# A gated linear attention and Mamba kernel: all transfers on one queue, issued by runs, and the weight check read again later

## The chip, the cores and the metric

The kernel runs on one core of a Trainium2 chip. The metric is the device time of one execution in microseconds; before the change it is 334.77 us (median of 3 runs, 333.81 to 335.59). The profile is one execution with a span of 334.8 us.

## The reference

```
# attention: batch 4, heads 8, seq 768, head_dim 48
for t in range(S):
    state = alpha[:, :, t, :, None] * state + np.einsum('bhd,bhe->bhde', k[:, :, t], v[:, :, t])
    y[:, :, t] = np.einsum('bhd,bhde->bhe', q[:, :, t], state)
# x: (4, 768, 384), the heads side by side; then the gated state space block
proj = x @ w_in                       # w_in 384 x 1024, float64
val, gate = proj[..., :512], proj[..., 512:]
h = a[0, 0] * h + val[:, t, :]        # one scan over t for each channel, a = exp(A_log)
out = (silu(gate) * h) @ w_out        # w_out 512 x 384, float64
```

Inputs q, k, v and alpha are float32; the two weight matrices come as float64, so each weight has 8 bytes, which the kernel turns into float32 itself with integer operations.

## The kernel before

**Tiles.** The sequence of each batch is cut into NG = 3 groups of 256 steps, so there are N = 12 groups ("turns" n = 0 to 11), three for each of the four batches. Within a group the recurrence is rewritten with running products of alpha: `front(n)` (L308) makes products V and P with scans on the vector engine (DVE; L339, L344), scales q and k by them (L353, L359), multiplies K and Q in blocks (sc, L368), masks (A, L371) and transposes K back (tpk, L142; copied to Kn by the scalar engine, ACT). `back(n)` (L385) makes block states z (L154) from Kn and v, adds them up to S_n (L393, L402), makes y from A and v (L169) and from S_n and Q (L187), copies y to x_sb on ACT (L410, L412), and transposes it (tpx, L196; copied to xT, L197). `ssm(n)` (L107) is the second block: four times the projections pj (L115, the value half and the gate half), the scan hh on DVE (L119), silu sg on ACT (L124), the product f on DVE (L125), and then twice the output product o (L130), copied to o_sb by ACT (L133) and stored.

**How q, k and alpha come in.** They have to lie with channels on partitions. For groups 0 to 3 they come as rows into the tile pads and are transposed by the matrix engine (tp, L326). For groups 4 to 11 they come as a batch (`load_batch`, L234): for each of a, q and k, several transfers copy 32x32 blocks, in memory runs of 32 or 16 numbers (128 or 64 bytes), and DVE transposes each block (`squares`, L329 and L330). Batch 1 is 48 transfers of 512 runs each; batches 2 and 3 are 12 transfers of 3072 runs each. The tiles of two batches share two buffers: batches 1 and 3 use big0, which at the start holds `staging`, the raw weights; batch 2 uses big1, which at the start holds pads.

**The weights.** 12 "units" (8 of w_in, 4 of w_out, 384 KB each) are fetched raw into staging (`fetch_unit`), and `convert_unit` (L270) makes float32 of each on ACT (L276, L277), DVE (L278, L280) and GpSimd (POOL, L282). The conversion holds only for weights in a certain range of size; `check_units(p)` (L284) tests that on ACT, three units at a time in place in staging, by a Square pass (L288) and a Relu pass (L289) with their sums in left_w. `check_products` (L377) tests the products V in the same manner. At the end `any_outside` reduces all of this to a flag; if it is set, a second slower program, `general`, runs. With these inputs it doesn't.

**What sets the order.** The order of each engine's instructions is written by hand: a string of letters for each turn. F steps front(n), A steps front(n+1), B steps back(n), P and H step ssm(n-1) (matmuls, then scan, silu and product), O steps ssm(n-2), which by then has only its two output products left, C checks products, U converts a unit, W checks units, L and M issue transfers:

```
467  early = ["FFFFLUFUFABBABB", "UUFPUUFHPUHFFPUHBBCPHABUAUBL", "FPUFHPUHFFPHBBCAPHBWAWOBWAWOM"]
468  usual = "FLPHPHFFOABBCPHABPHBAOM"
469  ending = ["PHPHOPHPHO", "OO"]
```

Each engine executes its instructions in this order, and each waits for its inputs and for its buffers. Transfers are issued by the sync engine (SP), which does nothing else, or by ACT, in whose stream an issue stands between computations. Before, SP issues pads, weights, the first four v and the batches; ACT issues the store of each o_sb (L134) and v of turns 4 to 11 (`load_last`, L483). `load_later` (L474) issues batches 2 and 3 at L of turns 3 and 5, and `load_last` batch 1 at M of turn 2, the whole batch at once. Pools matter too: the transposes tp, tpk and tpx share two PSUM buffers (ps_tp), pj and o share two (ps_mm), o_sb and xT have two each, v has three.

Of the kernel before, what the change touches and what calls it, by code (L numbers as in the profile page):

```python
# [9 lines left out]
FP32 = mybir.dt.float32  # L10
U8 = mybir.dt.uint8
U32 = mybir.dt.uint32
# [6 lines left out]
def kernel(  # L19
# [24 lines left out]
    nc = tc.nc  # L44
    B, H, S, D = q.shape
    DM = H * D
    DI = moe_A_log.shape[0]
    C = 128
    R = 64
    NR = C // R  # L50
    G = 2
    GC = G * C
    GR = G * NR
    NG = S // GC
    NP = H // 2
    DP = 64
    GP = G * NP
    NK = DM // C
    NI = DI // C
    N = B * NG  # L60
# [12 lines left out]
    w_out = const.tile([C, NI, DM], FP32, name="w_out")  # L73

    left = const.tile([C, N, 2], FP32, name="left")
    WP = 3
    left_w = const.tile([C, 3 * NI // WP, 2], FP32, name="left_w")
    flag = const.tile([1, 1], I32, name="flag")
    bias = const.tile([C, 3], FP32, name="bias")
# [3 lines left out]
    units = []  # L83
# [7 lines left out]
    def load_heads(dst, src, n, queue=nc.sync):  # L91

        b, g = divmod(n, NG)
        for c in range(G):
            rows = ds(g * GC + c * C, C)
            queue.dma_start(out=dst[:, c], in_=src[b, :, rows, :].rearrange("h p d -> p h d"))

    def load_pairs(dst, src, n, queue=nc.sync):

# [7 lines left out]
    def ssm(n, xT, prev_h, pool, ps_mm):  # L107

        b, g = divmod(n, NG)
        f = pool.tile([C, NI, GC], FP32, name="f")  # L110
        for cc in range(NI):
            pj = ps_mm.tile([C, 2, GC], FP32, tag="mm", name="pj")
            for i in range(2):
                for kk in range(NK):
                    nc.tensor.matmul(pj[:, i, :], w_in[:, kk, i, ds(cc * C, C)], xT[:, kk, :],  # L115
                                     start=(kk == 0), stop=(kk == NK - 1))
            yield
            hh = pool.tile([C, GC], FP32, tag=f"h{cc}", name="hh")
            nc.vector.tensor_tensor_scan(  # L119
                out=hh, data0=a_dec[:, cc:cc + 1].to_broadcast([C, GC]), data1=pj[:, 0, :],  # L120
                initial=prev_h[cc][:, GC - 1:GC] if g else 0.0, op0=ALU.mult, op1=ALU.add)
            prev_h[cc] = hh
            sg = pool.tile([C, GC], FP32, name="sg")
            nc.scalar.activation(sg, pj[:, 1, :], AF.Silu)  # L124
            nc.vector.tensor_mul(f[:, cc, :], sg, hh)  # L125
            yield
        for c in range(G):
            o = ps_mm.tile([C, DM], FP32, tag="mm", name="o")
            for cc in range(NI):
                nc.tensor.matmul(o, f[:, cc, ds(c * C, C)], w_out[:, cc, :],  # L130
                                 start=(cc == 0), stop=(cc == NI - 1))
            o_sb = pool.tile([C, DM], FP32, name="o_sb")
            nc.scalar.activation(o_sb, o, AF.Copy)  # L133
            nc.scalar.dma_start(out=out[b, ds(g * GC + c * C, C), :], in_=o_sb)  # L134
            yield

    def keys_back(K, Kn, ps_tp):
# [66 lines left out]
    def ranged(ctx):  # L204
        def pool(name, bufs, **kw):
            return ctx.enter_context(tc.tile_pool(name=name, bufs=bufs, **kw))

        own = pool("own", 1)
        p1 = pool("p1", 1)
        p2 = pool("p2", 2)  # L210
        p3 = pool("p3", 3)
# [18 lines left out]
        W = 32  # L230
        NW = S // W
        batches = {}

        def load_batch(b):  # L234
            t = big.tile([C, 3, NP * NW * W], FP32, tag=f"big{1 - b % 2}", name="batch")
            for m, (name, src) in enumerate((("a", alpha), ("q", q), ("k", k))):
                tv = t[:, m].rearrange("p (x e) -> p x e", e=W)
                batches[b, name] = t[:, m].rearrange("p (j x) -> p j x", j=NP)
                w0 = max(0, BY_VECTOR - NG * b) * GC // W
                for i in range(2):  # L240
                    nc.gpsimd.memset(tv[ds(DP * i + W, W), :, D - W:W], 1.0 if name == "a" else 0.0)  # L241
                for j, nj in [(0, NP)] if w0 == 0 else [(j, 1) for j in range(NP)]:
                    for i in range(2):
                        for half in range(2):
                            ch = min(W, D - W * half)
                            nc.sync.dma_start(  # L246
                                out=tv[ds(DP * i + W * half, W), j * NW + w0:(j + nj) * NW, 0:ch],
                                in_=src[b, ds(NP * i + j, nj), w0 * W:S, ds(W * half, ch)]
                                .rearrange("j (w p) d -> p (j w) d", p=W))

        vs, st, xs = {}, {}, {}

        def load(n, names="aqkv", queue=nc.sync):
            for name in names:
                if name == "v":
                    vs[n] = p3.tile([C, G, H, D], FP32, name="v_sb")
                    load_heads(vs[n], v, n, queue)
                elif n < BY_VECTOR:
                    load_pairs(pads[n % NBUF][name], dict(a=alpha, q=q, k=k)[name], n, queue)

        staging = big.tile([C, len(units), NK * C * 2], U32, tag="big0", name="staging")
# [19 lines left out]
                                           op0=ALU.bitwise_and, op1=ALU.bitwise_or)  # L281
            nc.gpsimd.tensor_add(units[u][0].bitcast(I32), units[u][0].bitcast(I32), lo.bitcast(I32))  # L282

        def check_units(p):  # L284


            h = staging[:, ds(WP * p, WP), :].rearrange("p u (x two) -> p (u x) two", two=2)[:, :, 1].bitcast(FP32)
            nc.scalar.activation(h, h, AF.Square, scale=2.0 ** -16, accum_out=left_w[:, p, 0:1])  # L288
            nc.scalar.activation(h, h, AF.Relu, scale=-2.0 ** 60, bias=bias[:, 0:1], accum_out=left_w[:, p, 1:2])  # L289

# [86 lines left out]
        def check_products(n):  # L377
            V = Vs[n % 2]
            junk = p1.tile([C, NP, GC], U8, name="junk")
            nc.scalar.activation(junk, V[:, :, 0:GC], AF.Relu, scale=-1.0 / LOW, bias=bias[:, 0:1],  # L380
                                 accum_out=left[:, n, 0:1])
            nc.scalar.activation(junk, V[:, :, 0:GC], AF.Relu, scale=1.0 / HIGH, bias=bias[:, 2:3],
                                 accum_out=left[:, n, 1:2])
# [58 lines left out]
        for u in range(4, 8):  # L442
            fetch_unit(u)
        nc.scalar.activation(a_dec, a_log, AF.Exp)
        to_convert, to_check = iter(range(len(units))), iter(range(len(units) // WP))

        def any_outside():

            worst = own.tile([C, 1], FP32, name="worst")
            bad = own.tile([C, 3 * NI // WP * 2 + 1], FP32, name="bad")  # L450
            nc.vector.tensor_reduce(out=bad[:, 0:1], in_=left.rearrange("p n w -> p (n w)"),
# [12 lines left out]

        early = ["FFFFLUFUFABBABB", "UUFPUUFHPUHFFPUHBBCPHABUAUBL", "FPUFHPUHFFPHBBCAPHBWAWOBWAWOM"]
        usual = "FLPHPHFFOABBCPHABPHBAOM"
        ending = ["PHPHOPHPHO", "OO"]
        fronts = {n: front(n) for n in range(N)}  # L470
        backs = {n: back(n) for n in range(N)}
        ssms = {}

        def load_later(n):  # L474
            if n < 2:
                load(n + 2)
            if n == 0:
                for u in range(8, len(units)):
                    fetch_unit(u)
            if n in (NG, 2 * NG - 1):  # L480
                load_batch(2 if n == NG else 3)

        def load_last(n):  # L483
            if n == 2:
                load_batch(1)
            if 2 <= n < N - 2:
                load(n + 2, "v", nc.scalar)

        with tc.manual_schedule():
            for n in range(N + 2):  # L490
                if n == N:
                    any_outside()
                for word in early[n] if n < len(early) else usual if n < N else ending[n - N]:
                    if word == "F":
                        step(fronts[n])
                    elif word == "A":
                        step(fronts.get(n + 1))
                    elif word == "B":
                        step(backs[n])
                    elif word in "PH":  # L500
                        if n - 1 not in ssms:
                            ssms[n - 1] = ssm(n - 1, xs.pop(n - 1), prev_h, p2, ps_mm)
                        step(ssms[n - 1])
                    elif word == "O":
                        step(ssms[n - 2])
                    elif word == "C":
                        if n == 1:
                            check_products(0)
                        check_products(n)
                    elif word == "U":  # L510
                        convert_unit(next(to_convert))
                    elif word == "W":
                        check_units(next(to_check))
                    elif word == "L":
                        load_later(n)
                    elif word == "M":
                        load_last(n)
            outside = nc.values_load(flag[0:1, 0:1], min_val=0, max_val=1)
        return outside

# [189 lines left out]
```

## Time and profile before

| engine | busy us | share of span |
|---|---|---|
| PE (matrix) | 291.8 | 87% |
| DVE (vector) | 223.5 | 67% |
| ACT (scalar) | 126.0 | 38% |
| POOL (GpSimd) | 45.0 | 13% |

PE busy is the time in which a matmul is under way; PEld is the loading of its weights, which overlaps. The page also gives, for 40 equal slices of the span, the busy share of each engine in tenths, the clock that was granted to PE, and the load of the 16 DMA engines. Of 134,784 packets of SP's queue and 22,736 of ACT's, nearly all are under 512 bytes. The chain of waits follows the work that ended last back to its start; 75% of the span in it is PE, 6% DVE, 6% DMA, 5% ACT. The last turn's work ends with 24 matmuls of o and the store of the last o_sb.

### The profile page before, as it was taken

The numbers are of one execution on the slowest core, as the hardware profiler recorded it, in microseconds if no ns is written. First come the engines' busy times: TensorE is split into PE (matmuls) and PEld (weight loads), VectorE is DVE, ScalarE is ACT, GpSimd is POOL, SyncE is SP. The second block draws the span as 40 slices with busy tenths as digits, with TensorE's granted clock in tenths as the row PEclk, the third lists the DMA queues.
The fourth block names the chain that finished last, engine by engine and source line by source line (L and its number), as shares of the span: only waits on it lengthen the run. The fifth ranks groups of instructions, "written<-read, shape, count | busy, mean of one in ns | idle before, by whom it ended". The sixth has DMA issues, their size and how long they took to land.

```text
span 334.8 us, 9254 instructions
## 1 busy us (share of the span) xinstructions
PE 291.8 (87%) x4041; PEld 231.6 (69%) x4041; DVE 223.5 (67%) x387; ACT 126.0 (38%) x259; POOL 45.0 (13%) x58
## 2 busy tenths in 40 slices
PE   1577995899499792599999999999999999999993
PEld 1355883787377671477787778877887778777771
DVE  1886786769123960679878888898788988833220
ACT  1133668237932410243252442513524325244111
POOL 4020420320069300000910000000000000000000
PEclk9995898699789898599999999999999999999999
DMA  9999994000056547976885996940030120000011
GB/s 129 224 223 239 204 222 86 0 3 4 23 104 99 72 74 99 125 101 94 116 117 108 132 120 99 153 79 31 2 72 25 28 46 25 25 26 2 27 45 59
DMA packets 157570, 29.01 MB, mean 87 GB/s; under 512 B 150864, under 2 KB 157008, under 8 KB 157520
## 3 DMA queue, kind: packets, MB, share of 16 engines
q1 hardware_dynamic: 134784, 20.06, 41.2%
q10 hardware_dynamic: 22736, 8.26, 10.1%
q8 instruction: 34, 0.56, 0.7%
q14 instruction: 16, 0.13, 0.1%
HBM read 23.60 MB, written 4.72 MB: 85 GB/s over the span
## 4 chain that ended last, share of the span: by engine, by line
PE 75%; DVE 6%; DMA 6%; ACT 5%; SPq 3%; issue 3%; ACTq 1%; DVEq 0%
PE pj L115 34%; PE o L130 18%; PE sc L368 4%; PE tp L326 4%; PE tpk L142 4%; PE y L187 4%; PE z L154 3%; PE y L169 3%; DMA v_sb<-in_v_dram 3%; PE tpx L196 3%; SPq L246 2%; DVE P L344 2%; DVE V L339 2%; DMA pads<-in_alpha_dram 1%; DMA batch<-in_q_dram 1%
## 5 line engine op out<-in xcount | busy, mean ns | idle before, releaser
L115 PE MATMUL pj<-xT,w_in 128*128 128x256 f32 x576 | 135.6, 389 | 0.0
L115 PEld LDWEIGHTS pj<-xT,w_in 128*128 128x128 f32 x576 | 109.7, 194 | 17.6 <-issue 0.2
L130 PE MATMUL o<-w_out,f 128*128 128x384 f32 x192 | 67.9, 499 | 0.0
L124 ACT ACTIVATE sg<-pj 128x256 f32<-128x256 f32 x48 | 18.4, 384 | 119.1 <-DVE hh L119 98.6
L130 PEld LDWEIGHTS o<-w_out,f 128*128 128x128 f32 x192 | 36.2, 197 | 20.9 <-issue 2.1
L119 DVE TENSOR_TENSOR_SCAN hh<-a_dec,hh,pj 128x256 f32<-128x256 f32 x32 | 23.7, 740 | 21.1 <-PE pj L115 21.1
L125 DVE TENSOR_TENSOR f<-sg,hh 128x256 f32<-128x256 f32 x48 | 20.4, 425 | 24.9 <-ACT sg L124 24.9
L326 PE MATMUL tp<-ident,pads 128*128 128x128 f32 x96 | 19.6, 358 | 16.0 <-DMA pads<-in_alpha_dram 6.9
L241 POOL MEMSET batch<- 32x1536 f32 x18 | 24.7, 1371 | 64.7 <-DMA out_dram<-o_sb 41.7
L326 PEld LDWEIGHTS tp<-ident,pads 128*128 128x128 f32 x96 | 15.0, 183 | 19.4 <-issue 8.0
L368 PE MATMUL sc<-Q,K 64*64 64x64 f32 x768 | 15.9, 237 | 10.7 <-DVE K L359 10.6
L133 ACT ACTIVATE o_sb<-o 128x384 f32<-128x384 f32 x24 | 11.8, 490 | 33.5 <-PE o L130 33.5
L368 PEld LDWEIGHTS sc<-Q,K 64*64 64x64 f32 x768 | 14.0, 148 | 14.9 <-issue 14.3
L344 DVE TENSOR_TENSOR_SCAN P<-aT,iV,bias 128x256 f32<-128x256 f32 x32 | 23.6, 780 | 0.6
L339 DVE TENSOR_TENSOR_SCAN V<-aT,bias 128x256 f32<-128x256 f32 x32 | 20.3, 677 | 0.3
L393 POOL TENSOR_TENSOR S_n<-S_end,V 128x192 f32<-128x192 f32 x7 | 4.2, 598 | 118.5 <-DVE V L339 118.5
L330 DVE STREAM_TRANSPOSE K<-batch 128x1024 f32<-128x1024 f32 x8 | 9.9, 1239 | 12.7 <-DMA batch<-in_k_dram 12.7
L196 PE MATMUL tpx<-ident,x_sb 128*128 128x128 f32 x72 | 11.9, 300 | 6.0 <-DVE P L344 4.3
L187 PEld LDWEIGHTS y<-S_n,Q 64*64 64x64 f32 x704 | 13.1, 140 | 5.7 <-issue 4.9
L169 PE MATMUL y<-v_sb,A 64*64 64x48 f32 x768 | 14.2, 220 | 3.2 <-issue 3.2
L371 DVE COPY_PREDICATED A<-mask,sc 128x512 f32<-128x512 uint8 x24 | 16.1, 723 | 0.7 <-PE sc L368 0.7
L154 PEld LDWEIGHTS z<-v_sb,Kn 64*64 64x64 f32 x768 | 12.3, 134 | 6.1 <-issue 5.4
(64 smaller groups left out, 314.2 us busy)
## 6 DMA issues: line engine op xcount, KB each, us to landing
out_dram<-o_sb ACTq DMA_DIRECT2D x24, 192.0 KB, 2.0
staging<-in_moe_w_in_dram SPq DMA_DIRECT2D x8, 384.0 KB, 5.0
v_sb<-in_v_dram ACTq DMA_DIRECT2D x16, 192.0 KB, 3.4
pads<-in_alpha_dram SPq DMA_DIRECT2D x16, 96.0 KB, 5.0
pads<-in_k_dram SPq DMA_DIRECT2D x16, 96.0 KB, 3.7
v_sb<-in_v_dram SPq DMA_DIRECT2D x8, 192.0 KB, 4.4
staging<-in_moe_w_out_dram SPq DMA_DIRECT2D x4, 384.0 KB, 5.5
batch<-in_alpha_dram SPq DMA_DIRECT2D x4, 384.0 KB, 6.6
```

Of the source, the lines that this page charges most:

```text
L115: nc.tensor.matmul(pj[:, i, :], w_in[:, kk, i, ds(cc * C, C)], xT[:, kk, :], start=(kk == 0), stop=(kk == NK - 1))
L119: nc.vector.tensor_tensor_scan(out=hh, data0=a_dec[:, cc:cc + 1].to_broadcast([C, GC]), data1=pj[:, 0, :], initial=prev_h[cc][:, GC - 1:GC ...
L130: nc.tensor.matmul(o, f[:, cc, ds(c * C, C)], w_out[:, cc, :], start=(cc == 0), stop=(cc == NI - 1))
L154: nc.tensor.matmul(zv[chs, r, g, j, :], Kn[rows, g, j, chs], v_sb[rows, g, NP * i + j, :], start=True, stop=True, skip_group_check=True)
L169: nc.tensor.matmul(yv[at, i, c, j, :], A[rows, i, c * NP + j, :], v_sb[rows, c, NP * i + j, :], start=(c == 0 and j == 0), stop=False, ski ...
L187: nc.tensor.matmul(yv[at, i, c, j, :], Q[rows, j, ds(R * x, R)], S_n[rows, x, j, :], start=False, stop=(c == G - 1 and j == NP - 1), skip_ ...
L196: nc.tensor.transpose(tp[:, kk, :], x_sb[:, c, ds(kk * C, C)], ident)
L241: nc.gpsimd.memset(tv[ds(DP * i + W, W), :, D - W:W], 1.0 if name == "a" else 0.0)
L326: nc.tensor.transpose(tp[:, u, ds(c * C, C)], pad[name][:, c, j], ident)
L339: nc.vector.tensor_tensor_scan(out=V[:, 2 * jj + u, GC - 1::-1], data0=tp[:, u, ::-1], data1=bias[:, 1:2].to_broadcast([C, GC]), initial=1 ...
L344: nc.vector.tensor_tensor_scan(out=P[:, 2 * jj + u, :], data0=tp[:, u, :], data1=bias[:, 1:2].to_broadcast([C, GC]), initial=iV0[:, 2 * jj ...
L368: nc.tensor.matmul(scv[ds(R * r, R), i, c * NP + j, :], K[rows, j, steps], Q[rows, j, steps], start=True, stop=True, skip_group_check=True)
```

## The change

Three things are meant by it. All transfers of the main part after the first few go out on SP's queue, so that ACT issues none and no transfer of one queue has to wait for one of the other. The batches and v are no longer issued in one go: they are put on a list, `waiting`, and at each L, of which a usual turn has six, the head of the list is issued until 4096 memory runs (3072 from turn 4 on) are reached, so that stores and v find their way between the parts of a batch. And the check of the weights no longer reads staging in turn 2: staging is free for batch 1 as soon as the weights are converted, and the weights are fetched a second time, two units at a time, into a tile `part`, and checked in turns 6 to 11.

M now puts on the list what the next turns need (`make_ready`); G does what L did at first, loading pads of later groups and the last weight units. The strings change accordingly. check_products(0) goes from turn 1 to turn 0. In turn 2 the first projections go ahead of the q transposes of group 2, the first transposes of alpha of group 3 come right after tpk, ahead of the third projections, and all transposes of q of group 3 ahead of the first o; the number of matmuls is unchanged.

```diff
-    WP = 3
+    WP = 2
@@ load_heads
-            queue.dma_start(out=dst[:, c], in_=src[b, :, rows, :].rearrange("h p d -> p h d"))
+            pair = dst[:, c], src[b, :, rows, :].rearrange("h p d -> p h d")
+            if isinstance(queue, list):
+                queue.append(pair)
+            else:
+                queue.dma_start(out=pair[0], in_=pair[1])
@@ ssm
-            nc.scalar.dma_start(out=out[b, ds(g * GC + c * C, C), :], in_=o_sb)
+            nc.sync.dma_start(out=out[b, ds(g * GC + c * C, C), :], in_=o_sb)
@@
+        waiting = []
+
+        def issue(runs):
+            while waiting and runs > 0:
+                dst, src = waiting.pop(0)
+                nc.sync.dma_start(out=dst, in_=src)
+                runs -= src.size() // src.shape[-1]
@@ load_batch: nc.sync.dma_start(...) becomes waiting.append((...))
...
-        def check_units(p):
-            h = staging[:, ds(WP * p, WP), :].rearrange("p u (x two) -> p (u x) two", two=2)[:, :, 1].bitcast(FP32)
+        def fetch_part(p):
+            parts[p] = p1.tile([C, WP, NK * C * 2], U32, name="part")
+            for w in range(WP):
+                dst, src = units[WP * p + w]
+                waiting.append((parts[p][:, w].rearrange("p (a n) -> p a n", a=dst.shape[1]), src.bitcast(U32)))
+
+        def check_part(p):
+            h = parts.pop(p).rearrange("p u (x two) -> p (u x) two", two=2)[:, :, 1].bitcast(FP32)
@@
-        early = ["FFFFLUFUFABBABB", "UUFPUUFHPUHFFPUHBBCPHABUAUBL", "FPUFHPUHFFPHBBCAPHBWAWOBWAWOM"]
-        usual = "FLPHPHFFOABBCPHABPHBAOM"
+        early = ["FFFFGUFUFCABBABB", "UUFPUUFGHPUHFFPUHBBCPHABUAUB", "PFHPFUHUFFAPHBMBCPHALBAOLBOL"]
+        usual = "FLPHPLHFFOLABMBCLPHABLPHBAWLO"
@@
-        def load_last(n):
-            if n == 2:
-                load_batch(1)
-            if 2 <= n < N - 2:
-                load(n + 2, "v", nc.scalar)
+        def make_ready(n):
+            if n + 2 < N:
+                vs[n + 2] = p3.tile([C, G, H, D], FP32, name="v_sb")
+                load_heads(vs[n + 2], v, n + 2, waiting)
+            if 0 <= n - NG - 2 < len(units) // WP:
+                fetch_part(n - NG - 2)
+            if n in (2, NG, 2 * NG - 1):
+                load_batch({2: 1, NG: 2, 2 * NG - 1: 3}[n])
@@
-                    elif word == "W":
-                        check_units(next(to_check))
+                    elif word == "W" and n - NG - 3 in parts:
+                        check_part(n - NG - 3)
+                    elif word == "G":
+                        load_group(n)
                     elif word == "L":
-                        load_later(n)
+                        issue(4096 if n <= NG else 3072)
                     elif word == "M":
-                        load_last(n)
+                        make_ready(n)
```

## The prediction

> **What bounds the kernel now.** I read the 40 slices of the page first, to see whether one engine holds the whole span.
>
> ```profile
> PE   1577995899499792599999999999999999999993
> ACT  1133668237932410243252442513524325244111
> PEclk9995898699789898599999999999999999999999
> DMA  9999994000056547976885996940030120000011
> ```
>
> A slice is 8.37 us. From slice 17 on (about 144 us) PE is always at 9 at full clock: there the matrix engine is the bound and only a new hole can move it. Before that PE has holes, at slices 6, 10, 13, 15 and 16, and the digits of PEclk sag after each. The second view is busy time by stretch. I cut it at the start of each turn's projection matmuls (24 of them on pj, L115, in one run) and call those moments S3, S4, S5 and S6: 95.96, 121.90, 156.56 and 178.34 us in the chain of waits. The columns are the stretch, its length, PE, PEld, DVE, ACT, POOL busy (instructions), granted clock, DMA share, GB/s.
>
> ```profile
> 60.60:96.00 35.40, 30.84 (x375) 24.64 (x376) 19.44 (x37) 20.83 (x38) 5.17 (x5) 0.86 0.02 7
> 96.00:121.90 25.90, 23.94 (x320) 18.73 (x319) 16.60 (x29) 7.77 (x17) 15.59 (x12) 0.93 0.65 96
> 121.90:156.60 34.70, 24.13 (x336) 19.43 (x335) 18.33 (x32) 8.48 (x19) 0.00 (x0) 0.85 0.82 107
> 156.60:178.30 21.70, 21.70 (x335) 17.29 (x334) 18.30 (x30) 8.31 (x18) 9.04 (x7) 1.00 0.73 102
> ```
>
> A turn without a hole is 21.8 us of pure PE. Turn 3 took 25.9 and turn 4 34.7 for the same matmuls, and turn 2 moved almost no data (DMA 0.02). Third, the chain of waits in time order says who made the holes (start, length, what). First turn 2, then turn 4:
>
> ```profile
> 82.00 1.36 ACT staging L288 x2
> 83.38 1.43 ACT staging L289 x2
> 84.81 1.20 ACT staging L288 x2
> 86.06 1.18 issue
> 87.43 0.39 ACT o_sb L133
> ...
> 88.80 1.97 PE tp L326 x8
> 90.77 4.50 PE o L130 x8
> ```
>
> ```profile
> 123.08 0.40 ACTq L96
> 123.52 3.97 DMA v_sb<-in_v_dram
> 127.86 0.49 SPq L246
> ...
> 132.64 2.64 DMA batch<-in_k_dram
> 135.69 1.26 DVE K L330
> ```
>
> In turn 2 four weight checks (two pairs) stand on ACT between the copies of x_sb and o_sb, PE stops from 84.5 to 88.8, and then o takes 4.5 us instead of 2.58, because the clock is at half. In turn 4 PE has nothing from 127.2 to 137.8 because the k part of batch 1 lands at 135.3. It is late twice over: its transfers begin at 95 us, as soon as the last check of turn 2 has released the staging tile, and on the way they wait for transfers of the other queue. The list of SP's waits has that:
>
> ```profile
> SPq L246 <- ACT staging L289: 42.3, 1, 42.3
> SPq L246 <- DMA out_dram<-o_sb: 29.1, 7, 7.6
> SPq L246 <- DMA v_sb<-in_v_dram: 19.8, 7, 7.9
> ```
>
> The built instruction order explains the last two: eight semaphores go round over all transfers in program order, on both queues, so each transfer waits for the one eight places earlier. If that one is a store or a v load in ACT's stream, SP waits for ACT.
>
> **What the skill says.** "DMA: Bandwidth & Descriptors", section "Issuing engines are not separate DMA queues", says that transfers of all issuers share the same 16 engines and that several issuers only save issue time; so one queue should lose no bandwidth. The trace agrees as far as it goes: here two issuers cost SP up to 48.9 us of waiting. The same page, "Queues, rings and completion order", says that an engine consumes a queue's descriptors in ring order: a store behind a big load waits for it. No run here shows that yet. "TensorE: Matmul & The Clock Gate", Part 1, gives half clock after an idle window of about 3.4 us. The trace agrees: 0.50 from about 88 to 94.5 us after the 4.3 us hole, and 0.50 for about 3.2 us at 115 after a hole of only 1.7 us.
>
> **Part by part.** *Checks out of turn 2.* Twelve units in four pairs of passes cost ACT 4 x 2.7 = 10.8 us there (82.00 to 84.72 for a pair). They go. But I don't credit the whole hole, since the DVE is next. In turn 2 before, DVE ends the second P scan at 83.86, and Q needs it. Also check_products(0) goes from turn 1 to turn 0, where ACT waits anyway (fence, 21.3 us idle in all): 2.5 us of ACT gone from 51.5 to 54. There sg waited for it, then f, then V, so V starts 1.5 us earlier and turn 1 ends at about 59.0 instead of 60.6. The new order of turn 2 gives that back: pj comes ahead of the q transposes, so DVE idles about 2 us for Q; four transposes of the next a come right after tpk and need a buffer that ACT frees after Kn; and all eight q transposes stand before o, the second four behind that P scan (two tp buffers). Adding up DVE's list from Q (62.8) through hh, K, two conversions, the mask copy, two pairs of scans of 2.9 each and S_n, I get the end of P at 83.9 again. From there PE has half the q transposes 0.45, o 2.58, tpx 0.66, o 2.58, tp of k 0.87 = 7.15 us: S3 at 91.1 at full clock. The 2.5 us stop before it may cost up to 1.7 (half of one 3.4 us window); I take 0.4: S3 = 91.5, **gain 4.5**. Bounds: 89.5 if DVE keeps the 1.6, 93.5 if half clock lasts longer.
>
> *Batch 1 earlier and unhindered.* Its 48 transfers (512 runs each, 24,576 runs) need staging free of the last conversion (POOL, about 72), not of the checks. Behind v4, the first place of turn 2 issues four. Then a store stands in SP's order. It comes from o at about S3 - 4.1; eight follow, then the store at S3 + 0.2, then everything else is limited by SP alone. Nine such issues in a row took 127.86 to 132.11, 0.53 us each, and land 2.7 us later. So a is in at about S3 + 6, and DVE needs it at S3 + 8.1 (aT at 186.41 against 178.34). q: sixteen more, in at S3 + 14, needed at S3 + 20.8. k: four, a store (ready at S3 + 10.4), twelve, in at S3 + 23.4 = S4 + 1.6; needed between S4 + 1.3 (179.63) and, as sc starts at S4 + 5.2 and transpose and multiplication take 2.5, S4 + 2.7. So turns 3 and 4 run as a steady turn: 25.94 - 21.8 = **4.1** and 34.66 - 21.8 = **12.9**. The margin of k is only about 1 us.
>
> *Batches 2 and 3, v.* Batch 2 is 36,864 runs. Between 160 and 163 us the trace has 118 GB/s at a DMA share of 0.91; with 96 bytes a run on average (128 and 64 in turn) that is 0.81 ns a run, 30 us in all, from S4 on, needed a at S5 + 8.1, k at S6 + 1.3, 43 us later: hidden. v of turn n+2 is popped ahead of or behind a batch, always a turn before its z. Hidden.
>
> *Weights read again.* 12 units of 0.39 MB, 4.7 MB, 384 runs (w_in) each, in turns where the DMA digits are 0 to 3: hidden. ACT gets one pair of passes over 768 columns in each of turns 6 to 11, 2.72 less 2 x 384 x 0.85 ns = 2.05 us. Queued behind it is o_sb, and PE's second pj group of the next turn waits for o_sb's PSUM buffer. In the turn at 178, xT ends at 199.56, the pass would end at 201.6, o_sb at 202.1, and the second group is due at 202.5. Hidden by pj, with 0.4 us to spare; bounds 0 and 2.05 a turn.
>
> *Stores to SP.* ACT loses 24 issues of 0.36 us and 16 of about 0.5, off the path in PE-bound turns: nothing. The last store is issued by SP instead of ACT, after the same o_sb: nothing. The wait it adds: SP holds all later loads until o_sb, counted above.
>
> Sum: 4.5 + 4.1 + 12.9 = 21.5; 334.8 - 21.5 = 313.3, say **313.5**.
>
> **Rivals.**
> - *k is late still.* SP issued the sixteen q in 11.64 us, 0.73 each. For it: DMA shares are near 1 at times. Against: those had waits on the other queue. Then 40 x 0.2 = 8 us later, 7 us of hole and about 2.5 at half clock (sc 2.07 for 1.09, tpk 1.97 for 1.02, o 3.09): 323.
> - *The later checks stop PE.* The part lands late or o_sb's margin isn't there: 6 x 2.05 = 12.3, 325.8. Against: ACT is busy 8.3 of 21.7.
> - *Turn 2 follows PE, not DVE*, and all of the 1.6 us and the clock are kept: S3 at 88.5, 310.5.
> - *Slower.* Stores stand behind loads of 3072 runs in the one ring, o_sb (two buffers) isn't freed, and each of turns 3 to 11 waits one o of 2.58 us: 23.2, 336.7. For it: before, stores had their own queue and landed in 2.0 us. Against: a store has a whole turn before its buffer is wanted, and four loads ahead of it are about 10 us.
>
> **Numbers.** Forecast 0.60, late k 0.15, checks 0.08, turn 2 by PE 0.11, slower 0.05, and 0.01 about nothing. The range goes from 309 (below the fast turn 2) to 323 (late k included); checks and slower are left out. Faster 0.94, same 0.01, slower 0.05.
>
> **What would show it.** S3 near 91.5, S4 and S5 each 21.8 later, PE at 9 from slice 11 on; no wait of SP on a transfer of ACT's queue; the transposition of K (L352 of the changed kernel) starting within 2.7 us of S4; first pj group of turns 7 to 12 followed by the second without a hole. If S3 to S4 is over 23 us, a or q was late; if S4 to S5 is, k; if the turns after S6 exceed 21.8, the checks or the stores; if S3 is at 88, I overrated DVE in turn 2.

## The result, and the profile after

The changed kernel takes 324.91 us (median of 4 runs, 323.17 to 326.74) beside 335.18 us before (333.81 to 336.69): ratio 0.9693, 95% interval 0.9616 to 0.9770. It is faster by 10.3 us, where 21.5 was forecast; 324.9 lies 1.9 us above the top of the range. Run again, as a_again, it took 326.59 us (ratio 0.9725, 0.9658 to 0.9793). The profile shown here is of the run of 323.17 us, span 321.2; a_again's profile (span 325.0) is nearer to the typical run.

The 40 slices of the page, changed kernel (8.03 us each, counted from 0):

```profile
PE   1587995979799999999999999699999999998991
ACT  1065665135113515425225444325445445254120
PEclk9997997899799999999999999899999999999998
DMA  9998999101076699999999998613321300300001
```

Slices 13 to 16, where PE and its clock had fallen before, are full. There is a new gap at slice 25 (about 205 us), and the DMA line, which before fell to between 4 and 8 in places from 120 to 200 us, is at 9 without a break from slice 14 to slice 23.

The steps from one turn's 24 projections to the next, in the windows view. Columns as in the prediction: stretch, length, PE, PEld, DVE, ACT, POOL busy (instructions), granted clock, DMA share, GB/s.

```profile
90.90:112.80 21.90, 21.90 (x321) 17.42 (x320) 15.82 (x28) 7.79 (x17) 8.75 (x7) 1.00 0.70 99
112.80:135.20 22.40, 22.07 (x335) 17.49 (x334) 18.45 (x32) 8.16 (x18) 0.51 (x1) 1.00 1.12 127
...
200.60:227.00 26.40, 23.67 (x335) 18.45 (x334) 18.33 (x31) 10.76 (x23) 0.00 (x0) 0.94 0.36 95
227.00:248.80 21.80, 21.80 (x320) 17.35 (x319) 18.59 (x32) 9.94 (x23) 0.51 (x1) 1.00 0.27 74
270.60:293.90 23.30, 22.04 (x337) 17.30 (x336) 11.26 (x22) 11.92 (x27) 0.00 (x0) 1.00 0.16 53
```

The first two are turns 3 and 4, which took 25.9 and 34.5 before. The third is turn 8: 4.7 us over 21.8, with the clock at 0.94. The last is turn 11, 1.5 over. All marks beside the forecast (us; S3 is the start of the projections of turn 3, a turn runs from its projections to the next turn's, "end" is from the projections of turn 12 to the end of the span; every mark is read in the timeline):

| | S3 | turn 3 | turn 4 | turn 8 | turn 11 | end |
|---|---|---|---|---|---|---|
| before | 95.96 | 25.94 | 34.50 | 21.78 | 21.89 | 25.9 |
| forecast | 91.5 | 21.8 | 21.8 | 21.8 | 21.8 | 25.9 |
| changed | 90.87 | 21.92 | 22.44 | 26.46 | 23.31 | 27.3 |
| changed, again | 92.51 | 21.77 | 23.35 | 26.54 | 23.31 | 27.4 |

The forecast of each step gives a span of 313.4 (91.5, nine turns of 21.78, 25.9). Against it the second profile is later by 1.0 at S3, 1.55 in turn 4, 0.9 in turn 5 (22.71), 4.75 in turn 8, 0.3 in turn 10 (22.10), 1.5 in turn 11 and 1.5 at the end: 11.5, which gives 324.9 for its 325.0.

Turn 8 in the timeline of the changed kernel (start, length, engine, line, what; in brackets the idle time before and who ended it):

```profile
192.24 1.89 SPq L245 DMA_DIRECT2D batch<-in_k_dram  x1
194.23 2.51 SPq L245 DMA_DIRECT2D v_sb<-in_v_dram  x2
...
196.79 2.71 SPq L245 DMA_DIRECT2D part<-in_moe_w_in_dram  x2
...
203.53 0.91 ACT L310 ACTIVATE part<-part 128x768 f32<-128x768 f32 x1 [3.52 <-DMA part<-in_moe_w_in_dram]
...
205.52 0.47 ACT L137 ACTIVATE o_sb<-o 128x384 f32<-128x384 f32 x1
...
206.04 4.54 PE L119 MATMUL pj<-xT,w_in 128*128 128x256 f32 x12 [2.73 <-ACT o_sb L137]
```

Part 1 of the weights, the one checked at the end of turn 7, is issued behind the last k of batch 3 and behind v of turn 8, at 196.79. ACT is free for its check at 200.0, waits 3.52 us, copies o_sb only then, and PE's second group of projections waits 2.73 us for the buffer that o_sb reads. That group takes 4.54 us instead of 2.86, at half clock. So the 4.7 us of turn 8 are 2.7 of waiting and 1.7 of clock, and 0.3 around them.

The end of the changed kernel in its timeline: the reduction of the checks, and the last o_sb:

```profile
292.15 0.97 ACT L311 ACTIVATE part<-part,bias 128x768 f32<-128x768 f32 x1
...
293.25 0.17 DVE L476 TENSOR_SCALAR bad<-left_w 128x12 f32<-128x12 f32 x1 [2.22 <-ACT part L311]
...
293.77 0.27 PE L480 MATMUL wt<-ident,worst 128*1 128x128 f32 x1 [1.26 <-DVE worst L478]
...
314.81 0.49 ACT L137 ACTIVATE o_sb<-o 128x384 f32<-128x384 f32 x1 [2.09 <-PEq L700]
```

PE stands 1.26 us for a chain from the last check through DVE. From the end of the last o_sb, 315.3, it is 5.9 us to the end of the span; before it was 330.3 to 334.8, 4.5.

From SP's waits in the changed kernel (who waits, for whom: us in total, times, longest; three of the list's lines):

```profile
SPq L138 <- ACT o_sb L137: 66.9, 10, 12.1
SPq L245 <- ACT o_sb L137: 23.6, 3, 10.9
SPq L245 <- DMA part<-in_moe_w_in_dram: 2.8, 2, 1.6
```

No store and no v stands in the list as something SP waits for; the 29.1 and 19.8 us of before are gone. What is left of the late k, in turn 4 of a_again:

```profile
118.73 1.25 DVE L352 STREAM_TRANSPOSE K<-batch 128x1024 f32<-128x1024 f32 x1 [2.62 <-DMA batch<-in_k_dram]
...
120.84 1.44 PE L390 MATMUL sc<-Q,K 64*64 64x64 f32 x64 [1.22 <-DVE K L381]
```

### The profile page after: what moved, and what is told of

Same layout as the page of the kernel before. It is cut to its first block, busy times and chain, and to the rows that moved or that the text cites. A ratio compares the mean times of both kernels' runs of the same rounds, so it can differ in the third digit from the quotient of the medians.

```text
span 321.2 us, 9298 instructions
## 1 busy us (share of the span) xinstructions
PE 286.9 (89%) x4041; PEld 226.5 (71%) x4041; DVE 223.2 (69%) x387; ACT 126.3 (39%) x267; POOL 44.5 (14%) x58
## 5 line engine op out<-in xcount | busy, mean ns | idle before, releaser
L119 PEld LDWEIGHTS pj<-xT,w_in 128*128 128x128 f32 x576 | 109.8, 195 | 21.5 <-ACT o_sb L137 3.1
L134 PE MATMUL o<-w_out,f 128*128 128x384 f32 x192 | 67.3, 496 | 0.0
L348 PE MATMUL tp<-ident,pads 128*128 128x128 f32 x96 | 17.4, 327 | 15.4 <-DMA pads<-in_alpha_dram 7.1
L348 PEld LDWEIGHTS tp<-ident,pads 128*128 128x128 f32 x96 | 13.4, 167 | 18.5 <-issue 10.0
L390 PEld LDWEIGHTS sc<-Q,K 64*64 64x64 f32 x768 | 12.9, 137 | 5.3 <-issue 3.0
L390 PE MATMUL sc<-Q,K 64*64 64x64 f32 x768 | 15.0, 225 | 1.0 <-DVE K L381 0.6
L191 PE MATMUL y<-S_n,Q 64*64 64x48 f32 x704 | 14.2, 221 | 0.8 <-issue 0.6
L147 ACT ACTIVATE Kn<-tpk 128x512 f32<-128x512 f32 x24 | 13.0, 594 | 4.1 <-PE tpk L146 4.1
```

What stands on the lines that cost most here:

```text
L191: nc.tensor.matmul(yv[at, i, c, j, :], Q[rows, j, ds(R * x, R)], S_n[rows, x, j, :], start=False, stop=(c == G - 1 and j == NP - 1), skip_ ...
L348: nc.tensor.transpose(tp[:, u, ds(c * C, C)], pad[name][:, c, j], ident)
L390: nc.tensor.matmul(scv[ds(R * r, R), i, c * NP + j, :], K[rows, j, steps], Q[rows, j, steps], start=True, stop=True, skip_group_check=True)
```

## The experiments

All start from the changed kernel. Executions differ at the start by up to 3 us (last section), so steps between marks are compared first, and times as ratios to the kernel before on the same chip. The cuts of the edits leave lines out at "..." and where the text says so.

**1. The late part alone (e_head).**

```diff
-            parts[p] = p1.tile([C, WP, NK * C * 2], U32, name="part")
+            parts[p] = p2.tile([C, WP, NK * C * 2], U32, name="part")
-                waiting.append((parts[p][:, w]...
+                waiting.insert(w, (parts[p][:, w]...
```

> The changed kernel with one difference: the weights for a check go to the head of the list of waiting transfers, ahead of the rest of batch 3 (and have two buffers, so that this is free of a clash). In the changed kernel the matmuls of turn 8 to those of turn 9 take 26.46 us instead of 21.8: the check on ACT waits 3.52 us for its part, o_sb waits behind the check, and PE behind o_sb. Theory A, the part is only late: that turn goes back to about 21.8, the end comes 4.7 us earlier, about 320. Theory B, the two passes of the check on ACT (about 2 us) are themselves too long for the turn: the stretch stays above 23.5 us and other turns with a check (6, 7, 9 to 11) are above 21.8 too; 323 or more.

A part has two buffers here (p2), so that it can be fetched early. Turn 8 takes 21.78 us, and no wait of PE for o_sb over 0.5 us is left anywhere after turn 2. Turns 9 and 10, which follow a check too, take 21.8. Turn 7 took 23.04, though not for the check: PE stopped 0.95 us in the middle of a group of y without waiting for anything that the profile shows. 322.37 us, ratio 0.9616 (0.9546 to 0.9685); the span is 4.7 us below a_again's. Theory A holds for turn 8: the two passes, 2 us together, fit when their data is there, and lateness was the whole loss.

**2. Why it is late: load or place (e_early).**

```diff
+        first_L = [16384]
-                        issue(4096 if n <= NG else 3072)
+                        issue(first_L.pop() if n == 2 and first_L else 4096 if n <= NG else 3072)
```

> The changed kernel, but the first place of turn 2 issues 16384 runs instead of 4096, so 28 transfers of batch 1 instead of 4, in the stretch from 70 to 87 us in which SP stands before a store and the DMA engines are idle. Theory A, a backlog of the DMA engines from 112 to 202 us makes part 1 late (its transfers are issued at 196.8): everything behind comes 5 to 10 us earlier, part 1 is there before ACT asks for it at about 200, turn 8 takes 21.8 instead of 26.5 us, 4.7 us gained, about 320. Theory B, the places of the list in the turns set it and not the engines' load: part 1 is issued within 2 us of 196.8 and the time stays at 325. In both the projections of turns 3, 4 and 5 stay within 0.6 us of 90.9, 112.8 and 135.2.

Turn 4 takes 21.78 us, turn 8 23.04, and the time is 320.68 us, ratio 0.9495 (0.9396 to 0.9594). But part 1 is issued at 196.02, as theory B had it. Turn 8 in this kernel's timeline:

```profile
203.78 0.93 ACT L310 ACTIVATE part<-part 128x768 f32<-128x768 f32 x1 [1.75 <-DMA part<-in_moe_w_in_dram]
...
206.32 2.86 PE L119 MATMUL pj<-xT,w_in 128*128 128x256 f32 x12 [0.99 <-ACT o_sb L137]
```

SP is no longer behind here: from 147 us on most stores are issued in 0.36 us, the moment that their o_sb is there. Yet part 1 still comes only 6.55 us ahead of the projections of turn 8 (202.57), since batch 3 has 36,864 runs and a place 3,072: twelve places, two whole turns, all ahead of part 1. In the changed kernel it is 3.8 us ahead. So the backlog of the engines adds 2.8 us of lateness, and the rest is the place in the list. Both theories were partly right.

The same transfer stands 4.65, 4.55 and 5.05 us ahead in e_ofirst, e_endtail and e_half below; PE's wait there is 2.08, 1.59 and 1.80 us, against 2.73 at 3.8 us, 2.81 at 4.35 (a_again) and 0.99 at 6.55: the later, the longer, with some spread.

**3. Only the checks moved (e_twoq).**

```diff
-            nc.sync.dma_start(out=out[b, ...], in_=o_sb)
+            nc.scalar.dma_start(out=out[b, ...], in_=o_sb)
-                load_heads(vs[n + 2], v, n + 2, waiting)
+                load_heads(vs[n + 2], v, n + 2, nc.scalar)
                 load_batch({2: 1, NG: 2, 2 * NG - 1: 3}[n])
+                issue(1 << 30)
```

> The changed kernel with the old issuing: stores and v on ACT's queue, each batch issued at once where it is put on the list. The checks stay where the change has put them. This leaves only the move of the checks. Theory A, as my prediction has it: the two queues hold each other up (SP waited 48.9 us before for stores and v), so k of batch 1 is late in turn 4 again: the step from the projections of turn 4 to those of turn 5 is over 26 us, the time 328 or more. Theory B, the late release of the staging tile was the whole cause, and one queue was not needed: turns 3 and 4 take 21.8 to 22.5 us each. Then, with batch 3 issued at once, part 1 is in time too and the last store is ACT's again: 4.7 and 1.4 us less than the changed kernel, about 318.

333.94 us, ratio 0.9956 (0.9923 to 0.9989): almost nothing is left of the gain. Turn 4 takes 27.27 us and turn 8 31.0. SP's waits, and the late k in the timeline of this kernel:

```profile
SPq L245 <- DMA out_dram<-o_sb: 37.8, 9, 7.4
SPq L245 <- DMA v_sb<-in_v_dram: 16.2, 6, 7.2
```

```profile
117.01 1.25 DVE L352 STREAM_TRANSPOSE K<-batch 128x1024 f32<-128x1024 f32 x1 [4.37 <-DMA batch<-in_k_dram]
```

Batch 1 starts at 70 us, and k is late still, with SP waiting 54 us in all for stores and v of ACT's queue. Theory A holds: moving the checks is not enough. Part 1 is issued only at 203.46, and PE waits 6.06 us for o_sb, so turn 8 loses 9.2 us where turn 4 loses 5.5. This run undoes two things at once, the single queue and the issuing by runs. Which of them was needed, or whether either alone would do, was not run.

**4. Only the queue (e_checks2).**

```diff
-        early = [..., "PFHPFUHUFFAPHBMBCPHALBAOLBOL"]
+        early = [..., "PFHPFUHUFFAPHBBCPHABWAWOBWWOML"]   # W checks staging, three units
```

Only the line of the order is shown; no parts are fetched, and all else of the changed kernel stays.

> The changed kernel with its one queue and its list, but with the checks of the weights in turn 2, in place in staging, as before, and no second reading. This leaves only the queue. Batch 1 can then be issued only after the last check, at about 90 us. Theory A, the late release of staging was the cause of the hole in turn 4: projections of turn 3 at about 95.5 us, and the step from turn 4 to 5 still over 26 us; 330 or more. Theory B, the waits between the queues were the cause: 48 issues of 0.53 us, 25 us, put the last k at about 118 us, just in time; turns 3 and 4 take under 24 us each, no part is late and no check stands before the end: about 320 to 323.

328.82 us, ratio 0.980 (0.9728 to 0.9872), so whether 2% are reached is open. Neither theory has the turn right. Turn 4 takes 22.49 us; turn 3 takes 32.02. The waits of this kernel say why:

```profile
POOL batch L255 <- ACT staging L311: 21.9, 1, 21.9
DVE aT L352 <- DMA batch<-in_alpha_dram: 7.8, 1, 7.8
PE y L191 <- DVE S_n L422: 5.8, 1, 5.8
```

POOL cannot clear its part of the batch before the last check, a of batch 1 is issued from 98.2 us on, aT waits for it, and behind aT the scans, S_n and PE: the hole is the old one, met one turn earlier. From turn 5 on every step is 21.8 us and the step into turn 12 as well: without the second reading nothing is late. And S3 is at 92.75, with two pairs of checks on ACT ahead of it; the changed kernel in a_again has 92.51 with none. So with the new order of turn 2, which is in both, the checks no longer delay S3. They still hold an o_sb just behind it, for which PE waits 1.04 us in turn 3. What the move of the checks would bring in the old order was not run.

**5. The end (e_endtail).**

```diff
-                if n == N:
+                if n == N + 1:
                     any_outside()
-            nc.sync.dma_start(out=out[b, ...], in_=o_sb)
+            (nc.scalar if n == N - 1 else nc.sync).dma_start(out=out[b, ...], in_=o_sb)
```

> The changed kernel with two edits at its end: the reduction of all checks to the flag comes one turn later in program order, behind the last projections, and the stores of the last turn go out on ACT's queue. In the changed kernel the step from the projections of turn 11 to those of turn 12 is 23.31 us instead of 21.8 (PE waits for the reduction behind the last check), and from the end of the last o_sb to the end of the span it is 5.9 us against 4.5 before the change. Theory A, both are costs of the order of instructions: the step goes to 21.8 and the tail to 4.5, together 2.9 us. Theory B, the tail is set by how long the store takes to land, whoever issues it: the tail stays at 5.9. Theory C, for the step: the last check itself (ACT) holds o_sb and with it PE: the step stays over 22.5.

Turn 11 takes 21.78 us, and from the last o_sb (316.6) to the end of the span (320.9) it is 4.3. Theory A for both: 320.63 us, ratio 0.9533 (0.9495 to 0.9571). That is more than the 2.9 us expected; turn 8, at 23.64 with a shorter wait and full clock, took 2.8 less by itself.

The tail is not explained by the flag alone. Each engine reads the flag of `any_outside` once it is there and the engine's own work is done. Before, ACT was the last to read it, at 330.7, 0.4 us after its last o_sb; in the changed kernel it is SP, at 315.7, also 0.4 us after. The difference comes behind that reading: in all nine profiles where SP issues the last store, the span ends 5.3 to 5.6 us after SP's reading; in the five where ACT does, 3.9 to 4.9 us after ACT's. So the engine that issues the last store matters; why SP takes longer to finish is not shown.

**6. Turn 2, o first (e_ofirst).**

```diff
-        early = [..., "PFHPFUHUFFAPHBMBCPHALBAOLBOL"]
+        early = [..., "PFHPFUHUFFAPHBMBCPHALBOALBOL"]
```

> The changed kernel, but in turn 2 the first output product o stands ahead of the transposes of q of group 3 instead of behind them. In the changed kernel PE stands 2.52 us before the second half of these transposes (it waits for the second P scan on DVE), and the o that follows takes 4.44 us instead of 2.75, at half clock. Theory A (o does not need DVE and fills the hole): no hole over 0.5 us in turn 2 before the projections of turn 3, which come 2.5 to 4.2 us earlier, counted from the start of the hh scan at the last projections of turn 2 (77.44 us in the changed kernel, 13.43 before those of turn 3: 9.2 to 10.9 here). Theory B (DVE's list sets the end of turn 2 whatever the order): the hole only moves to the second half of q or to k, and the distance stays at 12.5 or more. Part 1 remains late in both.

The hole is gone. From the hh scan (81.69) to the projections (91.60) it is 9.91 us: 3.5 less than in the first profile of the changed kernel, but 1.8 less than in a_again (80.77 to 92.51), where the o behind the hole ran at full clock (last section). Turn 8 takes 25.82. 323.47 us, ratio 0.9617 (0.9576 to 0.9657). Theory A, at the lower size.

**7. What a batch costs (e_half).** Channels 16 to 31 of each head are left out in groups 4 to 11: as many runs, a third fewer bytes.

```diff
-                            ch = min(W, D - W * half)
+                            ch = D - W
```

> The changed kernel, but each memory run of a batch has 16 numbers: 64 bytes, where half of the runs have 128. It leaves out channels 16 to 31 of each head of alpha, q and k in groups 4 to 11. As many runs and transfers, two thirds of the bytes: 2.36 MB a batch for 3.54. In the changed kernel batch 3 takes 35.9 us from its first issue to its last (156.35 to 192.24), with five stores between. Theory A, the engines' time goes by runs, about 1 ns each whatever their length: still 33 us or more, part 1 late as before, turn 8 above 25 us. Theory B, it goes by bytes (about 118 GB/s in both): 25 us or less, SP then stands before stores and not before full rings, and turn 8 takes at most 23.1 us.

Batch 3 takes 34.05 us from first to last issue (161.31 to 195.36), against 35.9 in the first profile of the changed kernel and 34.5 in e_ofirst. The DMA view over this stretch, e_half (161 to 195 us):

```profile
DMA packets 34691, 3.38 MB, mean 99 GB/s; under 512 B 33749, under 2 KB 34686, under 8 KB 34686
```

and the changed kernel in a_again (158 to 194 us):

```profile
DMA packets 35773, 5.03 MB, mean 140 GB/s; under 512 B 34616, under 2 KB 35768, under 8 KB 35768
```

That is 1,020 and 994 packets a us, at 97 and 141 bytes each: the engines' time goes by packets, at 1.0 ns each. The places of the list do not set this pace: in both stretches SP stands in one issue after the other, up to 3 us for a transfer. Theory A holds; but turn 8 is 23.85 us and not above 25: its part came 5.05 us ahead of the turn, PE waited 1.80 us, and the clock stayed full (2.86 us for the 12 projections behind the wait, where e_ofirst has 4.54 behind 2.08).

**8. The second reading left out (e_noread).** No parts are fetched and none checked; their sums are set to zero.

> The changed kernel without the second reading of the weights and without their check: it leaves out that part of the computation (no transfers of parts, no passes on ACT, the sums of the check are set to zero at the start). The reduction to the flag stays where it was. Theory A, the second reading costs what the two steps show, 4.7 us in turn 8 and 1.5 in turn 11 (against 21.8), and nothing else: both steps go to 21.8, the rest stays, 6.2 us less than the changed kernel, 318.5 to 320.5. Theory B, the passes on ACT and the transfers also cost in the other turns: more than 6.2, under 318. Theory C, the load of batch 3 alone is enough for a hole in turn 8: that step stays above 23, 322 or more.

Turn 8 takes 21.78 and turn 11 21.89 us; 319.96 us, ratio 0.9460 (0.9397 to 0.9522). The ratio is 0.023 to 0.027 below that of the changed kernel, some 8 to 9 us, with an uncertainty of about 3; the two steps say 6.2. The times alone do not separate theory A from B. The steps speak for A: the second reading costs what it does in two places, and in turns 5 to 7, 9 and 10, at 21.8 to 22.0 us, nothing is gained without it.

**9. The changed kernel again (a_again), and its start with fewer weights in flight (e_calm).**

> The changed kernel itself once more, for its start. In its first profile PE has a hole of 0.65 us in the middle of the first y matmuls of turn 0 (it ends at 23.64 us), for which nothing that the profile shows is waited for; in seven of the eight kernels run since, with the same first turn, this hole is 3.9 to 4.1 us and ends near 27, and the projections of turn 3 come at 91.6 to 94.2 us instead of 90.9. Expected if that is a matter of the execution and not of the kernel: a hole of 3.9 to 4.1 us here, the projections of turn 3 at 93 to 94, the time again between 322 and 327. If the first profile is typical: 0.65 us and 90.9.

> The changed kernel, but the last four weight units (1.5 MB) are fetched in turn 1 instead of turn 0. In all profiles the hole in turn 0 ends 2 to 3 us after a packet of the instruction queue, which falls between 20 and 21 us where the hole is short and between 23 and 25 us where it is long; the DMA engines are at 9 in that stretch. Theory A, PE waits for its next block of instructions, and its packet stands behind the weights on the engines: with less on them the hole is under 1.5 us in the profile, and the times are 2 to 3.5 us below those of the changed kernel in the same call. Theory B, the hole has nothing to do with the load: 3 to 4 us as in the others, and the same times. If the units come too late for their conversion, turn 1 grows, and the gain at its end is smaller.

```diff
         def load_group(n):
+            if n == 1:
+                for u in range(8, len(units)):
+                    fetch_unit(u)
             load(n + 2)
-            if n == 0:
-                for u in range(8, len(units)):
-                    fetch_unit(u)
```

a_again has the long hole and S3 at 92.51, a little under what was expected. e_calm has it too, 3.86 us, and takes 325.36 us (ratio 0.9683, 0.9607 to 0.9758): no difference beyond the spread. Taking 1.5 MB of weights away from turn 0 does not shorten the hole; theory A in this form falls.

**10. All mends (b_all, b_all2).** Early issue of batch 1, o first, the reduction later, the last stores on ACT's queue, and each part fetched a turn earlier:

```diff
-            parts[p] = p1.tile([C, WP, NK * C * 2], U32, name="part")
+            parts[p] = p3.tile([C, WP, NK * C * 2], U32, name="part")
-            if 0 <= n - NG - 2 < len(units) // WP:
-                fetch_part(n - NG - 2)
+            if 0 <= n - NG - 1 < len(units) // WP:
+                fetch_part(n - NG - 1)
```

> All mends together: 28 transfers of batch 1 at the first place of turn 2, the first o of turn 2 ahead of the transposes of q, each weight part fetched a turn earlier (three buffers), the reduction of the checks behind the last projections, the last stores on ACT's queue. If the causes add up: from the projections of turn 3 on, each step is 21.8 us (no hole over 0.5 us), the projections of turn 3 stand 2.5 to 4.2 us earlier in the run, and the tail is 4.5 us; against the changed kernel 4.7 + 0.65 + 1.5 + 1.4 + 2.5 to 4.2 = 10.7 to 12.4 us less, so 312 to 315. If the load of the DMA engines is conserved and only moves the hole, one turn among 4 to 9 is still 23 us or more, and it comes to 316 to 320.

316.56 us (median of 6, 313.61 to 317.42), ratio 0.9415 (0.9379 to 0.9451). Slices of b_all:

```profile
PE   1484998698999999999998999999999999999993
PEclk9997699689999999999999999999999999999999
DMA  9999999102667799998999997906015000000101
```

From the projections of turn 3 on every turn is 21.8 us but turn 6 (22.94, a stop of 0.87 us that nothing in the profile explains), and the tail is 4.6. No part holds PE. Its span is 9.9 us below that of a_again, where 10.7 to 12.4 were expected: the mends hold, but o first brings 1.8 and not 2.5 to 4.2, and the stop in turn 6 is new. No hole has moved to another turn.

> All mends of the kernel before (316.56 us), the last four weight units in turn 1 as in the run above, and in turn 2 the third projections ahead of the first transposes of alpha of group 3, where PE stood 1.55 us for Kn. If both add up: 1.5 us from turn 2 and 2 to 3.5 from the start, 311 to 313. If DVE's list binds in turn 2 once PE's holes are gone, the 1.5 us do not show in the projections of turn 3; if the hole of turn 0 stays, 315 to 317.

With the last weights in turn 1, as in e_calm, and the third projections of turn 2 also ahead of the first transposes of alpha: 315.65 us (315.03 to 316.20), ratio 0.9439 (0.9389 to 0.9489). The 1.55 us stop is gone, and PE stands 0.67 us for a P scan instead; S3 is at 89.12, 2.6 us before b_all's. The hole of turn 0 is 4.14 us, and the tail, with ACT's store as in b_all, is 5.3. By the ratios it can't be told from b_all.

## Why the prediction was wrong, step by step

**Turns 3 and 4: right, in mechanism and nearly in size.** 17.0 us were forecast for both; the two profiles gave 16.1 and 15.3. (The forecast read S5 in the chain of waits, 156.56, and S3 and S4 in the timeline, where S5 is 156.40; there were 16.8 us to gain.) Undoing either half shows that both were needed: over 2 x 21.8 us, turns 3 and 4 lose 16.8 us before, 10.9 with the queue and the list alone, 5.6 with the move of the checks alone, 0.8 and 1.5 with both. The margin of k, "only about 1 us", was used up, in part because SP issued q at 0.60 us each and not 0.53: k was transposed 3.5 and 4.45 us after S4, where 2.7 was the limit. In the six later kernels that issue batch 1 like the changed one, turn 4 took 22.3 to 23.9 us, the longest with a stop without a wait in it. With 28 transfers issued earlier (e_early) that loss is nil.

**Checks out of turn 2: the number was met by luck, and its cause is only half shown.** S3 was forecast at 91.5 and came at 90.87 and 92.51. But the first of these had a short stop of PE in turn 0, 0.65 us, where the kernel before had 3.04 and a_again 3.59 (last section). Counted from the end of that stop, S3 comes after 69.6 us before, and after 65.0 to 67.3 us in the ten profiles with the changed order and a 2.5 us hole: a gain of 2.3 to 4.6, with the forecast 4.5 at its upper end. And e_checks2 gains as much with the checks still there. I counted the 10.8 us of checks as going from ACT's list; with the new order they no longer stood in the way of S3. DVE as the next limit was right: PE stood 2.52 us before the second half of the q transposes, for the P scan.

**"Weights read again, in turns where the DMA digits are 0 to 3: hidden": this step failed.** It cost 4.7 us in turn 8. I took the digits of the kernel before for turns that the change fills, and never worked out where in the list a part stands. Even in the kernel before, the digits are 0 to 4 only from slice 26 on; in slices 21 to 25, 176 to 218 us, turns 6 and 7, they are 5 to 9. Two turns of places, batch 3's, are ahead of part 1; and the engines are at 9 up to about 193 us, since batch 3 takes them about 35 us and not 30. The 0.81 ns a run was a peak over 3 us; over 35 us it is 1.0. The margin on ACT that I feared, "0.4 us to spare", held: in e_head, up to turn 10, and in b_all the turns behind a check take 21.8 to 21.9 us, but for one turn each with a stop of PE without a wait.

**The second cost was left out.** any_outside was not costed: the last check now comes just before it, and PE waits for both: 1.5 us. **"The last store is issued by SP instead of ACT, after the same o_sb: nothing" failed too**, by 1.4 to 1.5 us: the span ends later behind SP's reading of the flag than behind ACT's. These three terms, put at nothing, make 7.7 of the 11.5 us; late k, an S3 later by 1.0 and stops without a wait are the rest.

**The rivals.** "The later checks stop PE" gave 325.8 us, near what was measured, and names the part landing late. But its sum, 2.05 us in each of six turns, is not what happened: one turn lost 4.7, the other 1.5 stood at the end. "k is late still" happened, with 0.5 to 1.6 us in turn 4 where the rival had 9.5. "Slower" did not happen: stores did land later (median 3.9 us after 2.0), but no o waited for it. I put that to the ring, as the Trainium skill has it in "DMA: Bandwidth & Descriptors", section "Queues, rings and completion order": an engine consumes the descriptors of a queue in order. The runs do not show it. In e_checks2, with the one queue and less load, stores land in 2.1 us; in e_twoq, on their own queue but under load, in 2.8. That page's other section that I used says that transfers of all issuers share 16 engines and that a second issuer saves only issue time. The runs agree: between 178 and 200 us the kernel before, on two queues, moved 22,852 packets, 1,039 a us, against 994 on one queue in a_again, 4% fewer, and in e_twoq two queues cost SP 54 us in waits.

## What to carry to other kernels

When transfers go out from a list, work out for each item the place at which it leaves and what stands ahead of it there, and take the load of the engines from the list to come, not from the profile before. Something small with a due time belongs ahead of something big without one. Where a check or a reduction moves to the end, cost the chain behind it, and measure the end of the program for the engine that will issue the last store.

## What was not expected of the hardware

**Issuing takes longer while the engines are loaded.** A store's issue took SP 0.33 to 3.4 us in the changed kernel, median 0.43, and 2.1 to 3.4 us in the stretch from 125 to 192 us where the DMA digits are 9; on ACT, before, 0.34 to 0.39.

**Small packets cost 1.0 ns over 16 engines, at 97 as at 141 bytes on average** (e_half).

**A stop of PE without a wait.** In turn 0, in the middle of the first y, the first profile of the changed kernel and a_again have:

```profile
23.64 0.43 PE L173 MATMUL y<-v_sb,A 64*64 64x48 f32 x12 [0.65 <-issue]
```

```profile
26.67 0.66 PE L173 MATMUL y<-v_sb,A 64*64 64x48 f32 x12 [3.59 <-issue]
```

In fourteen profiles the stop was 0.65 and 0.93 us in the two where a packet of the instruction queue falls between 20 and 21 us, and 3.0 to 4.1 in the twelve where it falls between 23 and 25. It would fit an engine that waits for its next instructions, but that is only argued: e_calm, meant to free the way for that packet, has it between 23 and 24 us all the same and a stop of 3.86. It moves the start of the later turns by up to 3 us, and my first reading of S3 with it.

**Half clock after the same hole in some profiles and not in others.** "TensorE: Matmul & The Clock Gate", Part 1, gives an idle window of about 3.4 us. Behind 2.52 us of idle PE in turn 2 the two profiles of the changed kernel have, first and again:

```profile
82.48 4.44 PE L134 MATMUL o<-w_out,f 128*128 128x384 f32 x8
```

```profile
85.81 2.75 PE L134 MATMUL o<-w_out,f 128*128 128x384 f32 x8
```

Ten profiles have this hole, of 2.51 or 2.52 us with the same instructions around it: in four (the first of the changed kernel, e_calm, e_endtail, e_noread) o takes 4.44 us, in six 2.75. In turn 8 the clock was halved behind 2.08, 2.73, 2.81 and 6.06 us (4.54 to 5.49 us for 12 matmuls of pj), and not behind 0.99, 1.59, 1.80 and 2.06 (2.86). In the kernel before it was halved behind 1.74 us in turn 3 (4.54), a hole that the prediction counts as agreeing with the page; it does not, being half of that window. The same part calls the window free-running and the number of slow matmuls at a kernel's start run-variable, which leaves room for two outcomes of one hole. But these holes are shorter than the window. What the runs show is that from 1.7 to 2.5 us it goes either way; what decides stays open.
